# Attention and a squared-ReLU MLP on one core: the first pair in token halves, values behind scores, and more of the first product in batch 1

## The chip, the cores and the metric

The kernel runs on one NeuronCore of one Trainium2 chip. The metric is the device time of one execution in microseconds (us): the median of three runs, and lower is better. Before the change it is 417.86 us (417.58 to 418.33).

A core has five engines that run side by side, each with its own instruction stream that is worked off in order: TensorE (PE, matrix products; its weight loads are listed as PEld), VectorE (DVE, elementwise work), ScalarE (ACT, the exponentials), GpSimd (POOL) and SyncE (SP). The last two mostly issue transfers here. TensorE writes into PSUM, a small memory from which VectorE and ScalarE read; everything else lies in SBUF.

## The reference, cut to what matters

```python
batch, n_heads, seq, head_dim = (8, 12, 448, 64)
n_tokens, d_model, d_ff = (3584, 768, 2048)

def _attn_ref(q, k, v):
    scale = 1.0 / np.sqrt(q.shape[-1])
    scores = scale * np.matmul(q, k.transpose(0, 1, 3, 2))
    m = np.max(scores, axis=-1, keepdims=True)
    e = np.exp(scores - m)
    attn = e / (np.sum(e, axis=-1, keepdims=True) + np.exp(-m) + 1e-09)
    return np.matmul(attn, v).astype(np.float32)

def _moe_ref(x, w_in, w_out):
    h = x @ w_in
    r = np.maximum(h, 0.0)
    g = r * r
    return (g @ w_out).astype(np.float32)

# x: the attention's output, heads side by side: (8 * 448, 12 * 64)
```

Multiplied through by exp(m), the attention is exp(s) / (1 + sum exp(s)): the maximum is not needed, and the kernel computes it in this form. The product with `w_in` is called the first product here, the one with `w_out` the second or output product.

## The kernel before

The unit of the attention is a pair of heads [...]. Batch 0 is cut into two query ranges of 192 and 256 tokens, so that its first product can start early: units 0 to 5 are the six pairs with the first range, 6 to 11 the six pairs with the second, 12 to 17 the six pairs of batch 1. From unit 18 on the units run two at a time, with output-product steps between the score visits (the joined stage, batches 2 to 7).

The first three pairs of batch 0 are loaded as fp32 over the queues of SyncE and ScalarE, cast to fp16, and transposed by TensorE. All else arrives over GpSimd's queue, which casts during the transfer. `keep_warm` issues matmuls on zeros whose result nobody reads, so that TensorE's clock rises and stays up.

```python
def cast(b, pr):
    for name in "qk":
        f = flat.tile([P, 2, RUN, D], FP16, name=f"flat{name}")
        if b == 0 and pr == 0 and name == "k":
            nc.scalar.activation(out=f, in_=naturals[name, b, pr], func=AF.Copy)
        else:
            nc.vector.tensor_copy(f, naturals[name, b, pr])
        naturals[name, b, pr] = f

def transposes(b, pr):
    tp = mp_tile(FP16)
    for i, name in enumerate("qk"):
        for s in range(RUN):
            for h in range(2):
                nc.tensor.transpose(...)
    ...
    parts = (0, S // 2, S) if b == 0 and pr == 0 else (0, S)
    for x, y in zip(parts, parts[1:]):
        nc.vector.tensor_copy(qks[b][:, 0:2, pr * S + x:pr * S + y], tp[:, :, x:y])
```

A unit's scores come in two visits (`scores(u, et, 0)` and `scores(u, et, 1)`), each with half of the keys; the exponentials (ScalarE) follow from one of two PSUM buffers. `values` is the product of the exponentials with v; its result lies in `xp`, of which there is one buffer. `row_sums` adds up the exponentials on TensorE and makes the reciprocal on ScalarE (a Ln and an Exp). `normalise` multiplies the two on VectorE and so frees `xp`.

The first product is queued as tiles of single steps; `drain(ns)` issues steps until their nominal time is used up, `run(ins, n)` issues the rest of n tiles. The end of a tile is two VectorE instructions (maximum with 0, square). Up to the joined stage `mp` tiles rotate in three PSUM buffers.

```python
for i in range(2 * NPAIR):                      # units 0 to 11
    ...
    scores(u, et, 0)
    if i == 0:
        keep_warm(4)
    if i == NPAIR:
        values(units[i - 1], ...); rcp = row_sums(...); normalise(two, xp, rcp)
        queue(0, FIRST)
        share[0] = left() / (NPAIR + 2)
    if i in transpose_at:
        transposes(*transpose_at[i])
    if i == 0:
        cast(0, 2)
    if i > NPAIR:
        drain(share[0] * 0.45)
    scores(u, et, 1)
    if 0 < i < NPAIR:
        keep_warm(1)
    if i and i != NPAIR:
        ... row_sums, values(units[i - 1], ...)
    if i > NPAIR:
        drain(share[0] * 0.3)
    ... add_chunks, normalise, drain(share[0] * 0.25)

for i in range(2 * NPAIR, 3 * NPAIR):           # units 12 to 17
    ...
    scores(u, et, 0)
    if i in transpose_at:
        transposes(*transpose_at[i])
    ... (loads and staging of later batches)
    drain(left() * 0.5 if first else share[0] * 0.45)
    scores(u, et, 1)
    ... row_sums, values of the unit before
    drain(share[0] * 0.15)
    for step in range(3):
        add_chunks(u, et, es, half, step)
        drain(share[0] * (0.15, 0.1, 0.15)[step])
    ...
    normalise(done, xp, rcp)
    if first:
        queue(FIRST, S - FIRST)
        share[0] = left() / (NPAIR + 1.5)

# joined stage, two units a turn
    scores(ua, ea, 0); rows(11); scores(ua, ea, 1); ...; rows(11)
    scores(ub, eb, 0); ...; rows(10); scores(ub, eb, 1); ...
    for at in pending:
        if at not in rcps:
            rcps[at] = row_sums([units[at]], ...)      # first turn: unit 17
        values(...); normalise(...)
    ... transposes of two pairs of batch 2
    if pr == 0:
        run(ins, len(ins))                             # what is left of batch 0
        queue((b - 1) * S, S)
```

Of the kernel before, what the change touches and what calls it, by code (L numbers as in the profile page):

```python
# [15 lines left out]
def kernel(  # L16
# [9 lines left out]
    nc = tc.nc  # L26
# [45 lines left out]
    win_r = moe_w_in.rearrange("(c p) f -> p c f", p=128)  # L72
    wout_r = moe_w_out.rearrange("(c p) f -> p c f", p=128)

    whole, vns, qks, xts, naturals, stages = {}, {}, {}, {}, {}, {}

    def load_v(b, p0, p1):
# [5 lines left out]
    def load_natural(b, p0, p1):  # L83

        raw = b == 0 and p1 <= 3
        for n, r in (("q", q_r), ("k", k_r)):
            src = r[b, :, 2 * p0:2 * p1]
            if raw:
                if p0 == 0:
                    whole[n] = e_pool.tile([P, RUN * S], FP32, name="et")  # L90
                t = whole[n][:, p0 * 512:(p0 + 1) * 512].rearrange("p (h t d) -> p h t d", h=2, t=RUN)
                (nc.sync if n == "q" else nc.scalar).dma_start(out=t, in_=src)
            else:
                if p0 % 3 == 0:
                    whole[n] = nat.tile([P, NPAIR, RUN, D], FP16, name=f"{n}n{p0 // 3}")
                t = whole[n][:, 2 * (p0 % 3):2 * (p0 % 3 + p1 - p0)]
                nc.gpsimd.dma_start(out=t, in_=src)
            for pr in range(p0, p1):
                naturals[n, b, pr] = t[:, 2 * (pr - p0):2 * (pr - p0) + 2]
# [39 lines left out]
            )  # L139


    def cast(b, pr):
        for name in "qk":
            f = flat.tile([P, 2, RUN, D], FP16, name=f"flat{name}")
            if b == 0 and pr == 0 and name == "k":
                nc.scalar.activation(out=f, in_=naturals[name, b, pr], func=AF.Copy)
            else:
                nc.vector.tensor_copy(f, naturals[name, b, pr])
            naturals[name, b, pr] = f

    def transposes(b, pr):
        tp = mp_tile(FP16)
        for i, name in enumerate("qk"):
            for s in range(RUN):
                for h in range(2):
                    nc.tensor.transpose(tp[64 * h:64 * h + 64, i, P * s:P * s + P],
                                        naturals[name, b, pr][:, h, s, :], ident[0:P, 0:P])
        if b not in qks:
            qks[b] = qk_pool.tile([128, 3, COLS], FP16, name="qk")
        parts = (0, S // 2, S) if b == 0 and pr == 0 else (0, S)  # L160
        for x, y in zip(parts, parts[1:]):
            nc.vector.tensor_copy(qks[b][:, 0:2, pr * S + x:pr * S + y], tp[:, :, x:y])

# [226 lines left out]
    def left():  # L392
        return sum(t[0] for t in ins)
# [9 lines left out]
    def drain(ns):  # L403
        while ins and ns > 0:
            ns -= one(ins)
# [10 lines left out]

    transpose_at = {pr - 1: (0, pr) for pr in range(1, NPAIR)}
    for pr in range(NPAIR):
        transpose_at[NPAIR + 3 + pr] = (1, pr)
    transpose_at[16], transpose_at[17] = (2, 0), (2, 1)  # L420

    def keep_warm(n):
        wp = m_psum.tile([128, 512], FP32, name="mp")
        for _ in range(n):
            nc.tensor.matmul(wp, warm[:, 0:128], warm, start=True, stop=True)
# [15 lines left out]
        ess[i] = (es, half)  # L441
        return units[i], ets[i], es, half

    keep_warm(9)
    cast(0, 0)
    transposes(0, 0)
    keep_warm(3)
    cast(0, 1)


    for i in range(2 * NPAIR):
        u, et, es, half = begin(i)
        two = units[i - 2:i] if i and i % 2 == 0 else None
        if i % 2:
            xp = x_psum.tile([128, 512], FP32, name="xp")
        mode[0] = COLS2
        scores(u, et, 0)
        if i == 0:
            keep_warm(4)
        if i == NPAIR:  # L460
            values(units[i - 1], ets.pop(i - 1), xp, units[i - 1][3])
            rcp = row_sums(two, (ess.pop(i - 2)[0:1], ess.pop(i - 1)[0:1]))
            normalise(two, xp, rcp)
            queue(0, FIRST)
            share[0] = left() / (NPAIR + 2)
        if i in transpose_at:
            transposes(*transpose_at[i])
        if i == 0:
            cast(0, 2)
        if i > NPAIR:  # L470
            drain(share[0] * 0.45)
        scores(u, et, 1)
        if 0 < i < NPAIR:
            keep_warm(1)
        if i and i != NPAIR:
            if two and i < NPAIR:
                rcp = row_sums(two, (ess.pop(i - 2)[0:1], ess.pop(i - 1)[0:1]))
            values(units[i - 1], ets.pop(i - 1), xp, (i - 1) % 2 * units[i - 1][3])
            if two and i > NPAIR:
                rcp = row_sums(two, (ess.pop(i - 2)[0:1], ess.pop(i - 1)[0:1]))  # L480
        if i > NPAIR:
            drain(share[0] * 0.3)
        add_chunks(u, et, es, half, 1)
        if two and i != NPAIR:
            normalise(two, xp, rcp)
        add_chunks(u, et, es, half, 2)
        if i > NPAIR:
            drain(share[0] * 0.25)
        if i == NPAIR + 5:
            load_natural(2, 0, 3)  # L490
            for j in range(2):
                load_wout(0, j, 2)


    for i in range(2 * NPAIR, 3 * NPAIR):
        u, et, es, half = begin(i)
        prev = units[i - 1]
        first = i == 2 * NPAIR
        if not first:
            xp = x_psum.tile([128, 512], FP32, name="xp")  # L500
        mode[0] = COLS2
# [3 lines that stand above are left out]
        if i == 2 * NPAIR + 2:  # L505
            load_natural(2, 3, 6)
            for j in range(2):
                load_wout(HALF, j, 2)
            load_v(2, 0, 6)
            stage(3)  # L510
        drain(left() * 0.5 if first else share[0] * 0.45)
        scores(u, et, 1)
        if first:
            done = units[i - 2:i]
            values(prev, ets.pop(i - 1), xp, prev[3])
            rcp = row_sums(done, (ess.pop(i - 2)[0:1], ess.pop(i - 1)[0:1]))
        else:
            done = [prev]
            rcp = row_sums(done, (ess.pop(i - 1)[0:1],))
            values(prev, ets.pop(i - 1), xp)  # L520
        drain(share[0] * 0.15)
        for step in range(3):
            add_chunks(u, et, es, half, step)
            drain(share[0] * (0.15, 0.1, 0.15)[step])
        if i == 3 * NPAIR - 1 and ins and ins[0][0] < ins[0][1]:
            run(ins)
        normalise(done, xp, rcp)
        if first:
            queue(FIRST, S - FIRST)
            share[0] = left() / (NPAIR + 1.5)  # L530

# [11 lines left out]
    for c in range((NU - 3 * NPAIR) // 2):  # L545
        i = 3 * NPAIR + 2 * c
        b, pr = units[i][0:2]
        new = []
        for j in range(2):
            new.append(begin(i + j))  # L550
        (ua, ea, sa, ha), (ub, eb, sb, hb) = new
        scores(ua, ea, 0)
        rows(11)
        scores(ua, ea, 1)
        add_chunks(ua, ea, sa, ha, 0)
        rows(11)
        scores(ub, eb, 0)
        add_chunks(ua, ea, sa, ha, 1)
        add_chunks(ua, ea, sa, ha, 2)
        rows(10)  # L560
        scores(ub, eb, 1)
        add_chunks(ub, eb, sb, hb, 0)
        mode[0] = COLS2
        for at in pending:
            if at not in rcps:
                rcps[at] = row_sums([units[at]], (ess.pop(at)[0:1],))
            xp = mp_tile()
            values(units[at], ets.pop(at), xp)
            normalise([units[at]], xp, rcps.pop(at))
        add_chunks(ub, eb, sb, hb, 1)  # L570
        add_chunks(ub, eb, sb, hb, 2)
        if b in ON_PE and pr + 2 < NPAIR:
            transposes(b, pr + 2)
            transposes(b, pr + 3)
        if pr == 0:
            run(ins, len(ins))
            queue((b - 1) * S, S)
            if b > 2:
                run(outs)
            if b + 1 < B:  # L580
                transposed_loads(b + 1)
                hold(b + 1)
                load_v(b + 1, 0, NPAIR)
                if b + 2 < B:
                    stage(b + 2)

        n, early = ((3, 0 if b > 2 else 1), (7, 3), (6, 3))[pr // 2]
        run(ins, early)
        for at in (i, i + 1):
            rcps[at] = row_sums([units[at]], (ess.pop(at)[0:1],))  # L590
        run(ins, n - early)
        if pr == NPAIR - 2:
            complete(b * S)
        pending = [i, i + 1]
# [38 lines left out]
```

## Time and profile before

| | before |
|---|---|
| time, median of 3 | 417.86 us |
| span of the profiled execution | 415.9 us |
| TensorE busy | 405.5 us (98%) |
| VectorE busy | 278.8 us (67%) |
| ScalarE busy | 238.4 us (57%) |
| first exponential starts | 7.03 us |
| first exponential of unit 6 starts | 20.40 us |
| joined stage begins (scores of unit 18) | 67.35 us |
| last first-product steps of batch 0 | from 76.60 us |

A stretch of the profile gives each engine's busy time between two moments; the difference from the stretch's length is the engine's idle time. A line of a timeline gives the start and length of one or several instructions of the same kind, the tile written and the tiles read, the number of instructions, and in brackets how long the engine had been idle before and what released it. Matmuls are pipelined and their ends are modelled, so costs of TensorE are taken from differences of starts. The chain of waits is followed back from the last instruction: each of its pieces is what released the next. A transfer's line shows its issue; its landing is given separately, as the time from issue to landing.

### The profile page before, as it was taken

How to read it: one execution, taken by the hardware profiler on the slowest of the kernel's cores; microseconds unless marked ns; L12 is line 12 of the kernel's file. 1: busy time of each engine (PE TensorE's matmuls, PEld its weight loads, DVE VectorE, ACT ScalarE, POOL GpSimd, SP SyncE). 2: the span in 40 equal slices, each digit the busy share in tenths (PEclk: the TensorE clock that was granted, in tenths of full speed). 3: DMA queues.
4: the chain of work that ended last, by engine and by line, in shares of the span. 5: the costliest groups of instructions: out<-in, count | busy, mean ns of one | idle time of the engine just before them, and what ended most of it. 6: DMA issues, size and time to landing. Idle time of an engine off the chain costs nothing.

```text
span 415.9 us, 10695 instructions
## 1 busy us (share of the span) xinstructions
PE 405.5 (98%) x4721; PEld 256.7 (62%) x4721; DVE 278.8 (67%) x535; ACT 238.4 (57%) x329; POOL 36.4 (9%) x58
## 2 busy tenths in 40 slices
PE   8889999899999999999999999999999999999997
PEld 3567666566566666665666666665666666555664
DVE  4769888768865868568766769658676669287000
ACT  4897998664675664673576564674666655100111
POOL 7523220020000200002000400001000000000000
PEclk9999999999999999999999999999999999999999
DMA  9999999889109790199509871198101101010222
GB/s 201 197 197 198 200 197 223 159 120 199 40 2 182 139 192 6 44 199 191 123 2 164 167 151 37 39 186 154 46 2 39 39 2 39 39 39 0 77 76 77
DMA packets 75823, 45.58 MB, mean 110 GB/s; under 512 B 42560, under 2 KB 72000, under 8 KB 75456
## 3 DMA queue, kind: packets, MB, share of 16 engines
q0 software_dynamic: 28848, 22.16, 35.0%
q1 hardware_dynamic: 46208, 22.05, 23.3%
q8 instruction: 37, 0.61, 0.6%
q10 hardware_dynamic: 720, 0.69, 0.6%
q14 instruction: 10, 0.08, 0.1%
HBM read 45.69 MB, written 17.93 MB: 153 GB/s over the span
## 4 chain that ended last, share of the span: by engine, by line
PE 86%; DMA 9%; ACT 2%; DVE 2%; issue 1%; POOL 0%; POOLq 0%
PE mp L284 23%; PE mp L330 17%; PE mp L286 11%; PE xp L284 8%; PE sp L199 6%; PE xp L330 6%; PE mp L234 5%; DMA kn<-in_k_dram 4%; PE xp L286 3%; DMA win<-in_moe_w_in_dram 3%; PE xp L234 3%; PE sp L187 2%; DMA vn<-in_v_dram 2%; PE mp L248 2%; ACT et L167 1%
## 5 line engine op out<-in xcount | busy, mean ns | idle before, releaser
L167 ACT ACTIVATE et<-sp 112x896 f16<-112x896 f32 (+2 forms) x192 | 165.8, 914 | 55.6 <-PE sp L199 40.1
L284 PEld LDWEIGHTS <-win 128*64 128x64 f16 x1536 | 85.3, 110 | 45.7 <-issue 2.8
L284 PE MATMUL mp<-xt,win 128*64 128x448 f16 (+2 forms) x1236 | 110.2, 324 | 1.5 <-DVE xt L263 0.8
L330 PE MATMUL mp<-wout,gs 64*128 64x384 f16 x864 | 102.3, 322 | 0.0
L330 PEld LDWEIGHTS <-gs 64*128 64x128 f16 x1152 | 56.1, 94 | 31.7
L301 DVE TENSOR_SCALAR rt<-mp 128x448 f16<-128x448 f32 (+2 forms) x99 | 61.6, 622 | 17.4 <-PE mp L284 13.3
L303 DVE TENSOR_TENSOR gs<-rt 128x448 f16<-128x448 f16 (+2 forms) x128 | 50.2, 392 | 4.4
L330 PE MATMUL xp<-wout,gs 64*128 64x384 f16 x288 | 52.6, 322 | 0.0
L251 ACT ACTIVATE rcp<-mp,one_b 128x448 f32<-128x448 f32 (+2 forms) x40 | 25.1, 629 | 40.1 <-PE mp L248 35.8
L212 DVE TENSOR_TENSOR es<-et 112x896 f16<-112x896 f16 x42 | 26.0, 620 | 17.7 <-ACT et L167 17.6
L339 ACT ACTIVATE ot<-mp 128x384 f32<-128x384 f32 (+1 forms) x29 | 14.1, 487 | 36.2 <-PE mp L286 27.6
L199 PE MATMUL sp<-qk 64*112 64x224 f16 x480 | 33.8, 260 | 0.0
L286 PEld LDWEIGHTS <-gs 128*128 128x128 f16 x256 | 24.4, 98 | 15.1 <-issue 0.4
L284 PE MATMUL xp<-xt,win 128*64 128x448 f16 x300 | 32.6, 352 | 0.0
L199 PEld LDWEIGHTS <-qk 64*112 64x112 f16 x480 | 26.3, 128 | 9.7 <-issue 5.4
L234 PEld LDWEIGHTS <-vn 112*64 112x64 f16 x432 | 22.1, 109 | 15.3 <-issue 5.2
L286 PE MATMUL mp<-wout,gs 128*128 128x384 f16 (+1 forms) x192 | 31.0, 322 | 0.0
L341 DVE SCALAR_TENSOR_TENSOR ot<-mp,ot 128x384 f32<-128x384 f32 x27 | 15.1, 558 | 21.7 <-PE sp L199 11.6
L252 ACT ACTIVATE rcp<-rcp 128x448 f32<-128x448 f32 (+2 forms) x48 | 27.7, 577 | 1.5
L214 DVE TENSOR_TENSOR es<-es,half 112x896 f16<-112x896 f16 x42 | 26.2, 625 | 1.4
L212 DVE TENSOR_TENSOR half<-et 112x896 f16<-112x896 f16 x42 | 25.9, 616 | 0.3 <-ACT et L167 0.3
L301 DVE TENSOR_SCALAR rt<-xp 128x448 f16<-128x448 f32 x29 | 18.0, 622 | 12.0 <-PE xp L286 8.3
(61 smaller groups left out, 313.9 us busy)
## 6 DMA issues: line engine op xcount, KB each, us to landing
vn<-in_v_dram POOLq DMA_DIRECT2D x7, 672.0 KB, 9.0
out_dram<-ot SPq DMA_DIRECT2D x9, 384.0 KB, 2.8
win<-in_moe_w_in_dram POOLq DMA_DIRECT2D x8, 384.0 KB, 13.9
wout<-in_moe_w_out_dram POOLq DMA_DIRECT2D x4, 768.0 KB, 12.8
stage_q<-in_q_dram POOLq DMA_DIRECT2D x4, 676.0 KB, 10.9
stage_k<-in_k_dram POOLq DMA_DIRECT2D x4, 676.0 KB, 13.3
out_dram<-ot SPq DMA_DIRECT2D x8, 288.0 KB, 3.2
out_dram<-ot SPq DMA_DIRECT2D x9, 192.0 KB, 2.7
```

Source lines behind the costliest of these rows:

```text
L167: nc.scalar.activation(out=out_, in_=in_, func=AF.Exp, scale=scale)
L199: nc.tensor.matmul(sp[:, odd, h * (S // 2):(h + 1) * (S // 2)], qk[r, which, kx:kx + 2 * P - 1:2], qk[r, 0, x:x + S // 2], start=True, sto ...
L212: nc.vector.tensor_add((es, half[:, 0:2 * S])[step], e[:, 2 * step], e[:, 2 * step + 1])
L214: nc.vector.tensor_add(es, es, half[:, 0:2 * S])
L234: nc.tensor.matmul(xp[64 * h:64 * h + 64, o:o + n], vns[b][:, 2 * pr + h, kk, :], of_head(chunk(et, u, kk // 2, kk), u, h), start=(kk == 0 ...
L251: nc.scalar.activation(out=rcp[:, 0:m], in_=zp[:, 0:m], func=AF.Ln, bias=one_b)
L252: nc.scalar.activation(out=rcp[:, 0:m], in_=rcp[:, 0:m], func=AF.Exp, scale=-1.0)
L284: nc.tensor.matmul(out_[x:x + 64], lhsT[:, x:x + 64], rhs, start=start, stop=stop)
L286: nc.tensor.matmul(out_, lhsT, rhs, start=start, stop=stop)
L301: nc.vector.tensor_scalar(out=rt[:, 0:m], in0=hp[:, 0:m], scalar1=0.0, scalar2=None, op0=ALU.max)
L303: nc.vector.tensor_mul(gs[:, f0:f0 + per, t0 % RING:t0 % RING + n], r, r)
L330: nc.tensor.matmul(o[:, 0:w], g[x:x + 64], wout[x:x + 64, fb, n0:n0 + w], start=(fb == 0), stop=(fb == NFFB - 1))
```

## The change

It is meant to take idle time out of TensorE in the stages before the joined stage.

- Pair 0 is loaded, cast, transposed and copied in two halves of the tokens, so that the first scores need only the first half. Pair 2's keys move from ScalarE's queue to SyncE's. The casts of pair 1's keys move to ScalarE. There are four warm-up matmuls fewer.
- The values of units 2 and 4 are issued one unit later, after the next unit's first scores, so that scores don't stand behind values that wait for `xp`.
- Units 7 to 11 and 12 get fewer first-product steps, units 13 to 17 more, above all between the two score visits; batch 0's first product ends with unit 17, as do the row sums of unit 17. Two tiles of batch 1 instead of one then stand ahead of the first turn's row sums.
- Batch 1's pairs 3 to 5 are transposed one unit later.

```diff
+    HALVES = ((0, RUN // 2), (RUN // 2, RUN))
@@ load_natural
-                (nc.sync if n == "q" else nc.scalar).dma_start(out=t, in_=src)
+                for s0, s1 in HALVES if p0 == 0 else ((0, RUN),):
+                    eng = nc.sync if n == "q" or p0 == 2 else nc.scalar
+                    eng.dma_start(out=t[:, :, s0:s1], in_=src[:, :, s0:s1])
@@ cast, transposes: both take s0, s1
-            if b == 0 and pr == 0 and name == "k":
+            if pr < 2 and name == "k":
-        parts = (0, S // 2, S) if b == 0 and pr == 0 else (0, S)
+        for x, y in HALVES if b == 0 and pr == 1 else ((s0, s1),):
@@ before the loops
-        transpose_at[NPAIR + 3 + pr] = (1, pr)
+        transpose_at[NPAIR + 3 + pr + pr // 3] = (1, pr)
-    keep_warm(9)
-    cast(0, 0)
-    transposes(0, 0)
-    keep_warm(3)
-    cast(0, 1)
+    keep_warm(8)
+    cast(0, 0, *HALVES[0])
+    transposes(0, 0, *HALVES[0])
+    cast(0, 0, *HALVES[1])
+    keep_warm(2)
@@ units 0 to 11
         if i == 0:
-            keep_warm(4)
+            transposes(0, 0, *HALVES[1])
+            cast(0, 1)
+            keep_warm(1)
+            scores(u, et, 1)
+            keep_warm(1)
+        if two and i in (4, NPAIR):
+            values(two[0], ets.pop(i - 2), xp)
-            share[0] = left() / (NPAIR + 2)
+            share[0] = left() / (NPAIR + 4)
-        scores(u, et, 1)
+        if i:
+            scores(u, et, 1)
-            values(units[i - 1], ets.pop(i - 1), xp, (i - 1) % 2 * units[i - 1][3])
+            if i not in (3, 5):
+                values(units[i - 1], ets.pop(i - 1), xp, (i - 1) % 2 * units[i - 1][3])
@@ units 12 to 17
-        drain(left() * 0.5 if first else share[0] * 0.45)
+        before = 0.65 if i in transpose_at else 0.8
+        drain(share[0] * (1.2 if first else before))
-        drain(share[0] * 0.15)
+        after = 0.5 if first else 1.0 - before
+        drain(share[0] * after * 0.4)
-            drain(share[0] * (0.15, 0.1, 0.15)[step])
-        if i == 3 * NPAIR - 1 and ins and ins[0][0] < ins[0][1]:
-            run(ins)
+            drain(share[0] * after * 0.2)
+        if i == 3 * NPAIR - 1:
+            run(ins, len(ins))
+            rcps[i] = row_sums([u], (ess.pop(i)[0:1],))
-            share[0] = left() / (NPAIR + 1.5)
+            share[0] = left() / (NPAIR - 0.2)
@@ joined stage
-            if at not in rcps:
-                rcps[at] = row_sums([units[at]], (ess.pop(at)[0:1],))
-            run(ins, len(ins))
-        n, early = ((3, 0 if b > 2 else 1), (7, 3), (6, 3))[pr // 2]
+        n, early = ((3, 0 if b > 2 else 2), (7, 3), (6, 3))[pr // 2]
```

More of the change, by code (lines that the diff above doesn't have):

```diff
@@ L139, in transposed_loads, with cast, transposes @@
             )
-    def cast(b, pr):
+    fp16s = {}
+    def cast(b, pr, s0=0, s1=RUN):
         for name in "qk":
-            f = flat.tile([P, 2, RUN, D], FP16, name=f"flat{name}")
-            if b == 0 and pr == 0 and name == "k":
-                nc.scalar.activation(out=f, in_=naturals[name, b, pr], func=AF.Copy)
-            else:
-                nc.vector.tensor_copy(f, naturals[name, b, pr])
-            naturals[name, b, pr] = f
-    def transposes(b, pr):
+            if s0 == 0:
+                fp16s[name, b, pr] = flat.tile([P, 2, RUN, D], FP16, name=f"flat{name}")
+            f, t = fp16s[name, b, pr][:, :, s0:s1], naturals[name, b, pr][:, :, s0:s1]
+            if pr < 2 and name == "k":
+                nc.scalar.activation(out=f, in_=t, func=AF.Copy)
+            else:
+                nc.vector.tensor_copy(f, t)
+    def transposes(b, pr, s0=0, s1=RUN):
         tp = mp_tile(FP16)
[L153 to L157, printed above, removed]
         if b not in qks:
             qks[b] = qk_pool.tile([128, 3, COLS], FP16, name="qk")
-        parts = (0, S // 2, S) if b == 0 and pr == 0 else (0, S)
-        for x, y in zip(parts, parts[1:]):
-            nc.vector.tensor_copy(qks[b][:, 0:2, pr * S + x:pr * S + y], tp[:, :, x:y])
+        for i, name in enumerate("qk"):
+            for s in range(s0, s1):
+                for h in range(2):
+                    t = fp16s.get((name, b, pr), naturals[name, b, pr])
+                    nc.tensor.transpose(tp[64 * h:64 * h + 64, i, P * s:P * s + P], t[:, h, s, :], ident[0:P, 0:P])
+        for x, y in HALVES if b == 0 and pr == 1 else ((s0, s1),):
+            nc.vector.tensor_copy(qks[b][:, 0:2, pr * S + P * x:pr * S + P * y], tp[:, :, P * x:P * y])
     def exp(out_, in_):
```

## The prediction, made before the changed kernel ran

> **What bounds the kernel now.** I read four views in this order: busy time in stretches (where TensorE has gaps), TensorE's own timeline (what it waits for), the chain of waits (which transfers it passes through), and ScalarE's timeline. First the stretches; the columns are the stretch, its length, then the busy time of PE, PEld, DVE, ACT and POOL, the clock, the DMA share and GB/s.
>
> ```profile
> 5.05:19.90 14.85, 13.13 (x205) 7.88 (x204) 10.59 (x23) 11.35 (x17) 9.15 (x12) 1.00 1.41 207
> 19.90:27.86 7.96, 6.79 (x111) 4.91 (x108) 4.73 (x10) 7.42 (x10) 2.77 (x4) 1.00 1.45 197
> 42.00:67.35 25.35, 23.70 (x341) 16.23 (x338) 21.92 (x42) 23.84 (x33) 5.28 (x7) 1.00 1.38 206
> 67.35:83.11 15.76, 14.57 (x188) 9.51 (x186) 11.79 (x22) 10.69 (x15) 0.00 (x0) 1.00 0.87 177
> 83.11:355.60 272.49, 272.49 (x3267) 172.68 (x3266) 199.45 (x379) 164.83 (x226) 12.05 (x22) 1.00 0.49 96
> ```
>
> From 83.11 us on TensorE has no gap at all until the tail, and the change leaves that work as it is. So the time is what the first 83 us take, plus a constant, and only gaps, warm-up matmuls or work shifted within those 83 us can matter. Before that three engines take turns: ScalarE is busy 23.84 of 25.35 us while batch 1 runs alone. TensorE's timeline shows how it waits there and just after (start, length, instruction, idle before it):
>
> ```profile
> 19.48 0.52 PE L234 MATMUL xp<-et,vn 112*64 112x192 f16 x8 [0.79 <-DVE xt L263]
> 38.42 0.39 PE L156 MATMUL mp<-ident,kn 112*64 112x112 f16 x8 [0.28 <-DMA kn<-in_k_dram]
> 44.32 0.40 PE L187 MATMUL sp<-qk 64*112 64x448 f16 x2 [0.45 <-ACT et L167]
> 76.60 2.64 PE L284 MATMUL mp<-xt,win 128*64 128x256 f16 x36 [0.46 <-ACT rcp L251]
> ```
>
> The values wait behind a normalise, batch 1's second load arrives late, scores wait for a buffer that an exponential still reads, and after 75 us the last first-product tiles of batch 0 are all TensorE has while it waits for unit 17's row sums. The chain of waits shows that the loads form a second path through the first 38 us:
>
> ```profile
> 10.31 12.93 DMA win<-in_moe_w_in_dram
> 23.82 14.56 DMA kn<-in_k_dram
> ```
>
> The stretches have the DMA engines full at some 197 GB/s up to 42 us, so a faster start can't bring later data earlier. Landings, from the issues of short windows: keys of batch 1's first half at 26.8 us, of its second half at 38.4, its values at 41.9 (25.75 plus 16.1).
>
> [...] The first warm-ups here start 0.43 us apart, the three at 5.87 us take 0.82 together[...] Both queues already moved about half each of 340 GB/s between 3 and 5.2 us. [...]
>
> **Unit costs, from starts in TensorE's timeline.** One first-product step (two 64-column matmuls side by side): at 192 columns 12 matmuls go from 28.66 to 29.28, 0.103 us a step; at 256 columns 22 from 46.42 to 47.72, 0.118; at 448 columns 24 from 109.25 to 111.52, 0.189. A full set of transposes 0.42 (34.64 to 35.06), a half of batch 1's scores 0.52, values 0.75, row sums 0.22. On ScalarE a unit of batch 1 costs 4 exponentials at 0.87, a Ln and an Exp at 1.24: 4.7, and the units stand 4.81 apart (48.16 to 52.97).
>
> **Part 1, halves.** The first pair's queries are cast at 4.49, the first exponential starts at 7.03. With halves and 8 warm-ups TensorE is free at 1.20 + 8 x 0.427 = 4.62; the first half should have landed by then (4.45 now; half of both tensors is 229 KB less ahead of it, 0.67 us at the 340 GB/s of those two queues, so about 3.8). Transposes to 5.05, a half copy of 0.35 (two take 0.69 now), two warm-ups beside it, scores at 5.5, exponential at about 5.9: 1.1 earlier. The second starts at about 7.3 instead of 8.82, because the whole pair's second half no longer waits for VectorE's casts. Then the gain shrinks. Pair 2's casts, two half copies and unit 0's sums all queue on VectorE; its copy of pair 2 ends at about 10.6, against 11.2, so unit 2 starts 0.6 earlier. Four warm-ups fewer save 4 x 0.22, but they stood in waits.
>
> **Part 2, values behind scores.** At unit 6 it lets scores pass the 0.79 us wait, but ScalarE was idle for only 0.17 there. At unit 4 it may hurt: the values ran at 14.97 while TensorE would have waited for pair 4's copy anyway (scores at 15.77); now 0.44 of values stand between unit 4's two score visits, and I expect a ScalarE gap of up to 0.5. I keep **0.3 us** of gain at 20 us.
>
> **Part 3, fewer steps early.** Counting whole steps (a drain overshoots to a whole step): units 7 to 11 go from 13 to 11 each, unit 12 from 24 to 17, units 13 to 17 from 91 to 120, and the 12 left for after 75 us go to none. The sum is 192 in both. Units 7 and 8 are on ScalarE's path (its gaps there are under 0.2), units 9 to 11 on TensorE's (ScalarE gaps of 0.52, 0.55 and 0.53), so 10 steps, 1.03 us, bring 0.8: unit 12 starts at 37.23 - 1.1 = 36.1. Unit 12 lasts 4.78 now. It loses 7 steps (0.72), the transposes moved to unit 13 (0.42) and their wait (0.28): 3.4, so unit 13 starts at 39.5, after the 38.4 landing.
>
> **Part 4, batch 1 filled.** Unit 13: scores 1.04, transposes 0.42, 24 steps at 0.103, 4 at 0.118, values and sums 0.97: 5.4, with 0.4 of waits for exponentials 5.8, to 45.3. Units 14 to 16: 0.52 + 0.42 + 13 x 0.118 + 0.52 + 0.22 + 0.75 + 9 x 0.118 = 5.03 each, over ScalarE's 4.7, so TensorE becomes the bound and its waits go: 60.4. Unit 17 has 4 steps more, its own row sums and a wait for them: 5.8. The joined stage starts at 66.2, against 67.35: **1.15 earlier, with the 12 left-over steps already done**.
>
> **Part 5, joined stage.** It takes 15.76 us now. Its work to the end of the transposes is 8.8; less the row sums 8.6. Then two 448-column tiles, row sums, a third tile: 2 x 1.14 + 0.44 + 1.14 = 3.9. That is 12.5; I add 0.4, because ScalarE enters with two more Ln and Exp just before its exponentials. 12.9 instead of 15.76: 1.42 of steps gone, 0.22 of sums, and 1.2 of gaps (0.46, 0.35, 0.15, 0.22) as unit 17's reciprocal no longer queues behind eight exponentials. It ends at 79.1 instead of 83.1. Sum: **4 us less**, 417.86 - 4.0 = 413.9; I say 414.0.
>
> **Rivals.** (a) The loads bind. If the start gained more than 1.5 us, unit 9's transposes (28.27 now) would wait for the 26.8 landing; and unit 13's values, at about 43.3, cannot start before 41.9. So nothing brings the total down by more than about 1.4 us beyond my figure: about 412.4. For it: full DMA engines up to 42 us. Against: my start gains too little to reach it. (b) VectorE becomes the bound in batch 1. Per unit it has three adds at about 0.58, one normalise and one transposed copy at 0.54 each, and 1.83 tiles at 1.07 (51.99 to 53.06): 4.8 of 5.03 us. Because sums wait for the last exponential, tile evictions queue behind them, and with three rotating buffers TensorE could stall 0.2 to 0.4 per unit: 415 to 416. For it: 21.92 of 25.35 us busy already. (c) Longer drains between score visits starve ScalarE, and units stay at 4.8 plus the excess: 0.3 each, 1.5 in all: 415.5. Against: with 1.2 us of Ln and Exp still ahead of the next exponential, scores arrive early enough. (d) The second natural load of batch 2 waits for transposes one unit later and delays the second weight half. Against: the queue has work until 53.1, and the issue moves by about 1 us only; no change.
>
> **Range and chances.** (b), (c) and a lost start can each cost 1 to 1.5 us; (a) caps the other side at about 412.4, and my start and gap terms may be off by 0.7. So 411.8 to 416.4. A gain over 2% needs 8.4 us; the stretches from 5.05 to 83.11 hold 6.2 us of TensorE gaps in all (1.72 + 1.17 + 0.15 + 0.28 + 1.65 + 1.19), and the four warm-ups 0.9; a loss over 2% would need a new stall of 12 us. 0.02, 0.96, 0.02.
>
> **What would show it.** First exponential near 5.9 and second near 7.3; unit 6's first exponential 0.3 earlier than 20.40; no wait for keys at 38 us; units 14 to 16 about 5.0 apart with no TensorE wait for exponentials; no 256-column step after the first output product; the joined stage 12.9 long; the gapless stretch from about 79. The prediction is wrong if units of batch 1 stand over 5.3 apart, if unit 6 starts late, or if the gap after unit 17 persists in another form.

## The result, and the profile after

The changed kernel takes 421.5 us (median of 4 executions, 420.69 to 422.64) against 417.97 us for four of the kernel before (417.58 to 418.33): a ratio of 1.0087, 95% interval 1.0057 to 1.0116. It is slower by nearly 1%, where 414.0 was predicted and 411.8 to 416.4 given as the range.

The same stretches as before the change, from the changed kernel (stretch, length, busy time of PE, PEld, DVE, ACT and POOL, granted clock, DMA share, GB/s):

```profile
5.05:19.90 14.85, 12.60 (x136) 7.00 (x132) 7.54 (x18) 7.29 (x10) 8.70 (x11) 0.68 1.38 209
19.90:27.86 7.96, 6.78 (x81) 4.42 (x79) 4.12 (x9) 5.84 (x8) 3.30 (x4) 0.74 1.45 197
42.00:67.35 25.35, 24.99 (x400) 18.36 (x398) 23.47 (x46) 22.82 (x31) 7.73 (x10) 1.00 1.01 142
67.35:83.11 15.76, 13.68 (x180) 9.82 (x180) 10.66 (x20) 12.26 (x18) 0.00 (x0) 1.00 1.15 196
83.11:355.60 272.49, 272.33 (x3286) 172.84 (x3284) 199.77 (x379) 165.63 (x228) 11.77 (x22) 1.00 0.52 101
```

Read the clock column first: it was 1.00 in every stretch before, and is now 0.68 and 0.74 in the first two. In the first stretch TensorE is busy for 12.60 us with 136 matmuls, where it needed 13.13 us for 205. The stretches lie at the same times as before, but the work in them has moved: unit 12, the first of batch 1, starts at 42.89 us instead of 37.23, so the third line is batch 1 up to unit 16, and the fourth holds unit 17 and the start of the first joined turn. The third is fuller than before, 24.99 of 25.35 us. Finer stretches show where the clock goes:

```profile
9.00:10.00 1.00, 0.00 (x0) 0.00 (x0) 0.00 (x0) 0.47 (x1) 0.00 (x0) 1.00 1.35 227
10.00:11.00 1.00, 0.51 (x8) 0.29 (x8) 0.24 (x1) 0.86 (x2) 0.00 (x0) 0.67 1.42 203
12.00:24.00 12.00, 12.00 (x130) 7.47 (x130) 6.59 (x15) 7.40 (x10) 6.95 (x9) 0.50 1.46 197
24.00:25.00 1.00, 1.00 (x19) 0.66 (x15) 0.53 (x1) 0.83 (x2) 0.00 (x0) 1.00 1.45 196
```

TensorE stands still from 9 to 10 us; then the clock falls to one half, at 10.34 us, and stays there until 23.99. What it stood still for is in its timeline and in ScalarE's, in one piece of the chain of waits (start, length, what), and in the transfer's line, first of the kernel before, then of the changed one (size, time from issue to landing):

```profile
9.53 0.63 ACT L153 ACTIVATE flatk<-et 112x512 f16<-112x512 f32 x1 [1.91 <-DMA et<-in_k_dram]
10.07 0.79 ACT L172 ACTIVATE et<-sp 112x768 f16<-112x768 f32 x1
10.21 0.51 PE L165 MATMUL mp<-ident,flatk 112*64 112x112 f16 x8 [1.53 <-ACT flatk L153]
```

```profile
1.73 7.78 DMA et<-in_k_dram
```

```profile
et<-in_k_dram ACTq DMA_DIRECT2D x1, 224.0 KB, 5.2
et<-in_k_dram ACTq DMA_DIRECT2D x1, 224.0 KB, 7.8
```

Pair 1's keys, issued at 1.73 us, land at 9.5. Before, the same transfer took 5.2 us from an issue at about 1.2, so it landed at 6.4, and the transposes of these keys stood here in TensorE's timeline:

```profile
8.11 0.36 PE L156 MATMUL mp<-ident,flatk 112*64 112x112 f16 x8
```

ScalarE works in order: the cast of these keys, which the change put there, holds up unit 0's second exponential as well (10.07, predicted 7.3). It ends at 10.86, before the next scores start at 11.21, so it costs TensorE nothing; the late transposes do.

The second thing to see is at the end of batch 1, in TensorE's timeline, ScalarE's and VectorE's:

```profile
74.41 0.38 PE L253 MATMUL mp<-es,ones 112*64 112x448 f16 x2 [1.67 <-DVE es L219]
70.11 1.72 ACT L172 ACTIVATE et<-sp 112x896 f16<-112x896 f32 x2 [0.67 <-PE sp L192]
```

```profile
71.48 0.69 DVE L306 TENSOR_SCALAR rt<-mp 128x512 f16<-128x512 f32 x1 [1.35 <-PE mp L289]
72.20 0.42 DVE L308 TENSOR_TENSOR gs<-rt 128x512 f16<-128x512 f16 x1
72.55 0.62 DVE L217 TENSOR_TENSOR es<-et 112x896 f16<-112x896 f16 x1
73.08 0.62 DVE L217 TENSOR_TENSOR half<-et 112x896 f16<-112x896 f16 x1
73.73 0.63 DVE L219 TENSOR_TENSOR es<-es,half 112x896 f16<-112x896 f16 x1
```

Unit 17's row sums, now issued before the joined stage, wait 1.67 us for VectorE's three adds. These stand in VectorE's order behind a first-product tile that VectorE itself waits 1.35 us for, so the adds begin only at 72.55. The last two exponentials of the unit end at 71.83. Had the first add, which needs only the first two, run before that and the other two right after it, some 0.4 us of the wait would have been left (an estimate: 71.83 plus the 1.3 us from the second add to TensorE's start, less the 72.74 at which TensorE began to wait).

### The profile page after: what moved, and what is told of

Read it like the earlier page. It is cut to its first block, busy times and chain, and to the rows that moved or that the text cites. A ratio compares the mean times of both kernels' runs of the same rounds, so it can differ in the third digit from the quotient of the medians.

```text
span 420.9 us, 10694 instructions
## 1 busy us (share of the span) xinstructions
PE 409.7 (97%) x4717; PEld 260.2 (62%) x4717; DVE 278.5 (66%) x536; ACT 238.9 (57%) x331; POOL 36.2 (9%) x58
## 4 chain that ended last, share of the span: by engine, by line
PE 89%; DVE 4%; ACT 4%; DMA 2%; issue 1%; ACTq 0%
PE mp L289 24%; PE mp L335 16%; PE mp L291 10%; PE xp L289 7%; PE sp L204 6%; PE xp L335 6%; PE mp L239 5%; PE xp L239 4%; PE xp L291 4%; PE sp L192 3%; ACT et L172 2%; PE mp L253 2%; DMA et<-in_k_dram 2%; PE mp L165 2%; DVE qk L167 1%
## 5 line engine op out<-in xcount | busy, mean ns | idle before, releaser
L289 PE MATMUL mp<-xt,win 128*64 128x448 f16 (+2 forms) x1260 | 111.8, 324 | 0.8 <-DVE xt L268 0.8
L306 DVE TENSOR_SCALAR rt<-mp 128x448 f16<-128x448 f32 (+2 forms) x101 | 62.7, 621 | 23.8 <-PE mp L289 11.6
L335 PEld LDWEIGHTS <-gs 64*128 64x128 f16 x1152 | 57.1, 94 | 30.6
L344 ACT ACTIVATE ot<-mp 128x384 f32<-128x384 f32 (+2 forms) x29 | 13.9, 480 | 55.3 <-PE mp L291 44.2
L256 ACT ACTIVATE rcp<-mp,one_b 128x448 f32<-128x448 f32 (+2 forms) x38 | 23.9, 628 | 34.2 <-PE mp L253 34.2
L291 PEld LDWEIGHTS <-gs 128*128 128x128 f16 x256 | 24.4, 98 | 15.1 <-issue 0.4
L289 PE MATMUL xp<-xt,win 128*64 128x448 f16 x276 | 30.0, 352 | 0.1
L291 PE MATMUL mp<-wout,gs 128*128 128x384 f16 (+2 forms) x192 | 29.6, 313 | 0.0
L346 DVE SCALAR_TENSOR_TENSOR ot<-mp,ot 128x384 f32<-128x384 f32 x27 | 15.1, 558 | 18.9 <-PE sp L204 9.6
L192 PE MATMUL sp<-qk 64*112 64x448 f16 (+2 forms) x192 | 25.4, 342 | 2.1 <-ACT et L172 1.4
```

The lines of the kernel that those rows point to most:

```text
L192: nc.tensor.matmul(sp[:, h, o:o + n], qk[r, 1, x + P * kk:x + P * kk + P], qk[r, 0, x + q0:x + q0 + n], start=True, stop=True)
L289: nc.tensor.matmul(out_[x:x + 64], lhsT[:, x:x + 64], rhs, start=start, stop=stop)
L291: nc.tensor.matmul(out_, lhsT, rhs, start=start, stop=stop)
L306: nc.vector.tensor_scalar(out=rt[:, 0:m], in0=hp[:, 0:m], scalar1=0.0, scalar2=None, op0=ALU.max)
L335: nc.tensor.matmul(o[:, 0:w], g[x:x + 64], wout[x:x + 64, fb, n0:n0 + w], start=(fb == 0), stop=(fb == NFFB - 1))
```

## The experiments

Two questions were asked. Why does the start fail: is it the move of pair 2's keys, the halves, their short rows, or GpSimd's queue; and is it the late data or the clock that costs the time? And what are the other parts worth, where the sum of them promised nearly 4 us? All ratios are to the kernel before, with 95% intervals.

### Pair 2's keys back on ScalarE's queue

```diff
-                    eng = nc.sync if n == "q" or p0 == 2 else nc.scalar
+                    eng = nc.sync if n == "q" else nc.scalar
```

> The changed kernel, with pair 2's keys back on ScalarE's queue; pair 0 still in halves. In the changed kernel pair 1's keys landed at 9.53 us, TensorE stood idle for 1.53 us before them, and its clock was at half from about 10.7 to 24 us. Theory Q (the fourth and fifth load on SyncE's queue take the engines' turns from ScalarE's queue): pair 1's keys land near 6.5, no idle time over 1 us before 10 us, clock stays full, 415 us. Theory H (the halves double the number of rows of 512 bytes, so the two fast queues run dry or lag and GpSimd's queue comes in at 3.7 instead of 5.4): still near 9.5, half clock, 421 us.

Measured: 421.39 us, ratio 1.0082 (1.0054 to 1.011). Pair 1's keys land 7.9 us after an issue at about 1.7, as late as in the changed kernel, and the clock is 0.65 in the stretch from 5.05 to 20 us. Theory Q falls: moving the one transfer does nothing.

### Pair 0 loaded whole

```diff
-                for s0, s1 in HALVES if p0 == 0 else ((0, RUN),):
+                for s0, s1 in ((0, RUN),):
```

> The changed kernel, with pair 0 loaded whole (one transfer for q, one for k); casts, transposes and copies still in halves, pair 2's keys still on SyncE's queue. Theory H (the halves delay what follows): pair 0 lands near 4.5 and 4.9, pair 1's keys near 6.5, GpSimd's queue comes in at about 5.4, clock stays full, first exponential near 6.4, 414 to 415.5 us. Theory Q (the queue move): pair 1's keys still after 9, half clock, 420 to 421 us.

Measured: 417.07 us, 0.9993 (0.9972 to 1.0014). Pair 1's keys land 5.0 us after an issue at about 1.2, at 6.2; the clock is full in the profiled execution; GpSimd's first packets come at 5.2 us as before (5.4), not at 3.8. So the halved load alone brings the 4.4 us, and the rest of the new start, casts and copies in halves and four warm-ups fewer, makes no difference to the median. The first scores start at 6.08 us, but unit 6 at 20.02, against 19.94 in the kernel before. Of the 20 executions 16 took 416.74 to 417.51 us at full clock and two 418.33 and 418.49 at a mean clock of 0.996. The other two took 422.31 and 422.39, with a recorded clock of 1.0 and 0.999; no trace of them was kept, and their cause is open.

### Halves by head instead of by token

```diff
-                for s0, s1 in HALVES if p0 == 0 else ((0, RUN),):
-                    eng.dma_start(out=t[:, :, s0:s1], in_=src[:, :, s0:s1])
+                for h0, h1 in ((0, 1), (1, 2)) if p0 == 0 else ((0, 2),):
+                    eng.dma_start(out=t[:, h0:h1], in_=src[:, h0:h1])
```

> The changed kernel with pair 0 loaded in two halves by head instead of by token: as many transfers as in the changed kernel, but rows of 1024 bytes, as many rows as before. Theory R (the rows of 512 bytes, twice as many, delay what follows in the two fast queues): pair 1's keys land near 6.5, GpSimd's queue comes in after 5, clock full, about 417 us. Rival T (the number of transfers and their order do it): pair 1's keys after 9, half clock in most executions, 420 to 421.5 us. Casts and transposes of half the tokens need both heads, so the first exponential is no earlier than with the pair loaded whole.

Measured: 421.31 us, 1.0079 (1.005 to 1.0108). The rows are as long and as many as before, and still pair 1's keys take 7.3 us from an issue at about 1.7, landing near 9, where they take 5.0 with the pair loaded whole. Theory R falls: it is not the short rows but the splitting into more transfers, which makes pair 1's the third in their queues instead of the second.

### GpSimd's loads held until pair 1's keys have landed

```diff
-    load_v(0, 0, 3)
     ident = consts.tile([128, 128], FP16)
     make_identity(nc, ident)
+    landed = consts.tile([1, 1, 1, 1], FP32)
+    nc.gpsimd.tensor_copy(landed, naturals["k", 0, 1][0:1, 0:1, 0:1, 0:1])
+    load_v(0, 0, 3)
```

> The changed kernel with GpSimd's loads held back until pair 1's keys have landed (a one-element copy on GpSimd reads them); the loads of the two fast queues are unchanged. In both loads by halves the third transfer of each fast queue crawled, and GpSimd's packets came in just then (from 3.6 to 3.8 us, against 5.2 to 5.4 with pair 0 loaded whole). Theory P (GpSimd's packets take the turns): pair 1's keys land by about 6 us. Rival S (the third transfer of a fast queue is slow by itself, whoever else runs): they land after 8.5 us also with GpSimd's queue empty. The total says little, as all later data come later: 419 to 423 us.

Measured: 421.27 us, 1.0087 (1.0069 to 1.0104); the keys land 6.0 us after an issue at about 1.7, at 7.7. That lies between the two theories. Of the 3.1 us of lateness (9.5 against 6.4), GpSimd's packets explain 1.8. The other 1.3 us are there with GpSimd's queue empty, and the trace shows two slow places. Between 3.6 and 4.0 us, just after the four half transfers, both fast queues together move only 0.03 MB, where 0.4 us moved 0.12 before. And between 5 and 7 us SyncE's queue (q1) gets nearly all, while the last of pair 1's keys trickle in over ScalarE's (q10); packets, MB, share of the 16 engines:

```profile
q1 hardware_dynamic: 427, 0.41, 92.0%
q10 hardware_dynamic: 83, 0.07, 14.4%
```

SyncE's queue holds pair 2's keys here. Taking them off it did nothing while GpSimd's packets ran (7.9 us for pair 1's keys, against 7.8); with GpSimd's queue empty this was not tried. The cause of the 1.3 us is left open.

### Warm-up matmuls through the gap

```diff
             scores(u, et, 1)
-            keep_warm(1)
+            keep_warm(8)
```

> The changed kernel with seven more warm-up matmuls just ahead of pair 1's transposes, so that TensorE works while pair 1's keys are late; the loads are untouched, so the lateness itself stays. Theory C (the idle time costs most through the clock): the clock stays full, unit 6 starts near 22 instead of 26.0, total about 417.5 us. Rival (the late keys cost the time directly, the half clock is little beside it): unit 6 near 25 to 26, total 421 us or a little more.

Measured: 418.88 us, 1.0056 (1.0034 to 1.0079). Its first two stretches have their clock back:

```profile
5.05:19.90 14.85, 12.87 (x183) 7.02 (x180) 9.05 (x21) 8.99 (x13) 8.47 (x11) 1.00 1.37 207
19.90:27.86 7.96, 5.83 (x91) 4.18 (x87) 3.98 (x8) 7.47 (x11) 3.37 (x5) 1.00 1.45 197
```

The loads are as late as in the changed kernel, and yet 2.6 us are won by seven matmuls on zeros. The single executions show it more sharply, because seven matmuls did not always suffice: 12 of 20 had a mean clock of 0.999 or 1.0 and took 418.21 to 419.05 us, 8 had one of 0.984 to 0.988 and took 421.73 to 423.45. The half clock costs 3.9 us (422.5 less 418.6, the medians of the two groups), with the same instructions. A mean of 0.984 over 420 us is 13.4 us at half clock, which agrees with the 0.50 from 10.34 to 23.99 us above. In the changed kernel all four executions had 0.984 to 0.992, and so had all ten of the three versions before this one with the load in halves; of 91 executions of the kernel before only two fell below 0.999 (421.4 us at 0.984, 422.93 at 0.98). What is left at full clock, 418.6 against 416.9 with the pair loaded whole (medians of the executions at 0.999 or 1.0, without the two of 422 us), is the direct cost of the late keys: about 1.7 us.

### The old start with all the later parts

The edit puts the loads, casts, transposes and warm-ups of the first pairs back as they were and keeps everything else.

> The kernel before with all of the change but its start: loads, casts, transposes and warm-ups of the first pairs as before; values behind scores, fewer steps early, more steps in batch 1, row sums of unit 17 early. Theory: these parts work as predicted, and only the start failed: 413.5 to 414.5 us, unit 6 near 20.4, joined stage from about 67, gapless from about 79.5. Rival (VectorE or starved exponentials hold batch 1 up, or the wait of 1.67 us for unit 17's sums, seen in the changed kernel, eats it): 416 to 417 us.

Measured: 416.98 us, 0.9978 (0.9964 to 0.9993): the later parts bring 0.8 us, not nearly 4. The wait for unit 17's sums is here too, TensorE's timeline:

```profile
68.92 0.38 PE L249 MATMUL mp<-es,ones 112*64 112x448 f16 x2 [1.66 <-DVE es L215]
```

From unit 6 on this kernel and the changed one have the same lengths, to a few hundredths of a microsecond, in every stage; they differ in when unit 6 begins. So each stage can be set against the prediction (durations in us, from the first score visit of one unit to that of another; predicted ones from the terms of the prediction):

| stage | before | predicted | measured |
|---|---|---|---|
| units 6 to 11 | 17.29 | 16.5 | 16.87 |
| unit 12 | 4.78 | 3.4 | 3.73 |
| unit 13 | 5.71 | 5.8 | 5.42 |
| units 14 to 16 | 14.43 | 15.1 | 15.18 |
| unit 17 | 5.20 | 5.8 | 7.50 |
| first joined turn | 15.76 | 12.9 | 13.52 |
| sum | 63.17 | 59.5 | 62.22 |

### Unit 17's row sums where they were

```diff
-            rcps[i] = row_sums([u], (ess.pop(i)[0:1],))
@@ joined stage
         for at in pending:
+            if at not in rcps:
+                rcps[at] = row_sums([units[at]], (ess.pop(at)[0:1],))
```

> Old start plus the later parts (416.98 us), with unit 17's row sums put back to where the kernel before had them, behind the fourth score visit of the joined stage; batch 0's first product still ends with unit 17. Theory W (the early sums cost 1.66 us of TensorE idle time that the joined stage gives back only in part): the joined stage starts about 1.8 us earlier, but its first tile of batch 1 now waits some 1 to 1.5 us for the normalise behind eight exponentials: 416.0 to 417.0 us. Rival (the early sums are a clear net gain, they save the old 0.46 + 0.35 us of gaps and more): 417.5 us or more.

Measured: 416.45 us, 0.9964 (0.9952 to 0.9977): 0.5 us better than with the early sums. The early sums were a loss, but about half of the 2.05 us that their removal saves (unit 17 takes 5.45 us instead of 7.50) is given back in the joined turn, which takes 14.61 instead of 13.52.

### Unit 17's row sums in the middle

```diff
         rows(11)
+        for at in pending:
+            if at not in rcps:
+                rcps[at] = row_sums([units[at]], (ess.pop(at)[0:1],))
         scores(ua, ea, 1)
```

> Old start plus the later parts, with unit 17's row sums issued after the first eleven output steps of the joined stage: by then VectorE has the sums, so TensorE does not wait, and the reciprocal is still ahead of the other six exponentials. Theory W (the 1.66 us wait is a loss of order only): the wait goes and nothing takes its place, 415.2 to 415.6 us, 1.4 to 1.8 below 416.98. Rival (ScalarE or VectorE is the bound around the joint, and the wait shows up again at the score visits or tiles of the joined stage): 416.5 us or more.

Measured: 415.77 us, 0.9949 (0.9934 to 0.9963). The sums now come at 69.07 us, behind output steps that began at 67.16, and no idle time stands in the line:

```profile
67.16 1.95 PE L331 MATMUL mp<-wout,gs 64*128 64x384 f16 x22
69.07 0.38 PE L249 MATMUL mp<-es,ones 112*64 112x448 f16 x2
```

1.2 us are won over the early sums: unit 17 takes 5.46, the turn 13.98. Theory W holds for most of the wait; 0.46 us of it comes back in the turn.

### Values where they were

```diff
-        if two and i in (4, NPAIR):
-            values(two[0], ets.pop(i - 2), xp)
-            if i not in (3, 5):
-                values(units[i - 1], ...)
+            values(units[i - 1], ...)
```

> Old start plus the later parts, without values behind scores: units 2 and 4's values stand where the kernel before had them. If the part does what it is for, this is 0.2 to 0.5 us slower than 416.98. If, as the prediction feared, it costs a gap of ScalarE at unit 4, this is 0.2 to 0.5 us faster. If scores at units 4 and 6 wait for ScalarE's buffers anyway (0.94 and 0.90 us in the trace with the part), there is no difference, 416.8 to 417.2.

Measured: 416.55 us, 0.9971 (0.9959 to 0.9982): 0.4 us better without the part in the medians, though single executions overlap (416.13 to 417.08 against 416.46 to 418.19). ScalarE's timeline at unit 4, first with values behind scores, then with values in their old place:

```profile
16.80 0.81 ACT L168 ACTIVATE et<-sp 112x768 f16<-112x768 f32 x1 [0.46 <-PE sp L188]
17.94 0.81 ACT L168 ACTIVATE et<-sp 112x768 f16<-112x768 f32 x1 [0.34 <-PE sp L188]
```

```profile
16.45 1.63 ACT L168 ACTIVATE et<-sp 112x768 f16<-112x768 f32 x2 [0.46 <-PE sp L188]
```

The first gap of 0.46 us is there either way. The scores of unit 4 then wait for ScalarE's exponential, by the trace, but VectorE's copy of pair 4 ends at the same moment (16.33 us with the part, 15.98 without), so which of the two they wait for isn't shown; it is not the values, which stand behind these scores with the part. With the part a second gap of 0.34 us opens, since the values now stand between the two score visits.

### The corrections together

Old start, values in their old place, row sums in the middle:

> Old start, values where they were before, fewer steps early and more in batch 1, unit 17's row sums after the first eleven output steps. The gains of the two corrections were 1.2 us (415.77 against 416.98) and 0.4 us (416.55 against 416.98); if they add, 415.3 us, 2.4 below the kernel before. If one hides the other (ScalarE's gap at unit 4 is caught up by unit 9 anyway), 415.8 us.

Measured: 415.33 us, 0.9940 (0.9928 to 0.9953). The two corrections add, as the first case said. The same with the rest of the new start (casts, transposes and copies of pair 0 in halves, fewer warm-ups, pair 2's keys on SyncE's queue), the pair loaded whole:

> As the version just above, but with the start of the changed kernel (casts, transposes and copies of pair 0 in halves, pair 1's keys cast on ScalarE, eight and two warm-ups), pair 0 loaded whole. The prediction gave this start 0.3 us at unit 6. If so, 415.0 us, 0.3 below the version above. If the halves of the casts are worth nothing without the early landing, the same within 0.2 us. If fewer warm-ups let the clock drop in some executions, some of them lie 4 to 5 us above the rest.

Measured: 415.04 us, 0.9943 (0.9932 to 0.9954). The two can't be told apart. One of the latter's 20 executions had a mean clock of 0.983 and took 419.17 us; the others lie between 414.56 and 416.26. Both beat the kernel before and the changed one.

## Why the prediction was wrong, point by point

The prediction missed by 7.5 us (421.5 less 414.0). In the profiled execution 6.4 of this lie before unit 6, which started at 26.02 us where 19.64 was expected, and 2.7 in the stages up to the end of the first joined turn (62.22 less 59.5). That is 9.1; the profiled execution, at 422.64 us and so 8.6 above the prediction, was the slowest of the four. Two of the signs that the prediction named for being wrong came: unit 6 started late, and the gap after unit 17 persisted in another form.

**The step that failed is part 1, the halves.** Its first term was right and even cautious: the first half was cast at 3.38 us, where a landing at 3.8 was worked out. What it did not ask is what four transfers in place of two do to the transfer behind them. The working has no landing for pair 1, so this was left where the kernel before had it; it came 3.1 us later. The sentence that a faster start "can't bring later data earlier" looked in one direction only. Two consequences follow. TensorE resumes 2.1 us later than before (10.21 against 8.11, the transposes of pair 1's keys). And the clock falls after this gap, so that the work from there to unit 6 takes 15.8 us instead of 11.8: another 4.0. Together these are the 6.1 us by which unit 6 is late. The runs show the two separately: full clock by warm-ups is worth 3.9, data on time a further 1.7.

**The warm-ups were mis-sized as well.** "Four warm-ups fewer save 4 x 0.22, but they stood in waits" counted their time and not what they are for. The two beside the first copy were taken at the warm 0.22 each; in the profile they take 1.03 us together, as the first two of all do (from 1.20), where two of the kernel before take 0.60 from 5.87. By these lengths the clock had not risen yet, and the first exponential comes at 6.82 instead of 5.9. (The clock column reads 1.00 there; the cold start shows only in the lengths of the matmuls.) When the clock rises differed between two executions: with one and the same start unit 0's scores stand at 6.62 us in the profile of the kernel before, behind transposes of 0.39 us for a tensor, and at 7.23 in that with the later parts, behind transposes of 0.58. In the changed kernel it then fell: it went to 0.50 behind a gap of 1.53 us in sparse work (TensorE busy 1.71 of the 3.41 us before, 6.93 to 10.34), and 12 us of unbroken busy time passed before it rose. No rival in the prediction mentions the clock.

**Part 2** was sized nearly right in its doubt: "a ScalarE gap of up to 0.5" at unit 4 is 0.34, and taking the part out brings 0.4 us. The 0.3 of gain at unit 6 that was kept in spite of it was not there.

**Part 3** had the mechanism right. Units 6 to 11 gained 0.42 us where 0.8 was worked out, and unit 12 took 3.73 instead of 3.4, as its second scores still wait 0.19 us for an exponential. No wait for keys at 38 us remained, as expected.

**Part 4** was right for units 14 to 16: 15.18 us for three, or 5.06 each, against 5.03 worked out, and TensorE has no wait for exponentials in them. Rivals (b) and (c) did not come: VectorE kept up. For **unit 17** the term "its own row sums and a wait for them" was sized at about 0.3, of which less than 0.1 for the wait, and measured 1.97, of which 1.66 were the wait. The busy time of VectorE had been added up, but not the order in which its adds stand.

**Part 5** was short by 0.6: 13.52 instead of 12.9, among other things 0.41 us of waiting for a score buffer while ScalarE makes two more reciprocals.

**Rival (a)**, that the loads bind, was right about the resource and wrong about the place. It looked at GpSimd's queue at 27 and 42 us, where it made no difference, and not at the two fast queues at 4 us. (Its cap, 413.9 less 1.4, is 412.5 and not 412.4; nothing hangs on it.) **Rival (d)** did not come, as was argued there: the second weight half made nobody wait.

The sentence that a loss needs "a new stall of 12 us" stands for a loss over 2%; what came was a loss of under 1%, out of a stall of 2 us and the half clock that followed it.

## What to carry to other kernels

Cutting a load in two to start earlier can also delay what stands behind it in its queue (here 7.8 us from issue to landing instead of 5.2): look up when the next transfer's data are needed, and weigh the early half against that. Warm-up matmuls that fill a wait are an insurance against a low clock (here 1.00 instead of 0.68 in the first stretch, in the profiled execution): weigh them by what the clock would cost, not by what they take. Seven of them won 2.6 us in the late gap here, while the new start with four fewer made no difference to the median once the data were on time (417.07 against 416.98 us). Before a result is wanted earlier, read the order of the engine that makes it: its position behind other work on VectorE decided the wait here, and issuing the sums a few steps later was worth 1.2 us.

## What the runs showed of the hardware that was not expected

- A gap of 1.53 us in TensorE's work before 10.2 us was followed by 13.65 us at half clock (10.34 to 23.99), although TensorE was busy without a gap for 12 of them. The price was 3.9 us; whether it was paid varied between executions of one kernel with the gap partly filled (8 of 20).
- The low clock lasted 13.65 us in the changed kernel's profile, and the other times fit multiples of a quarter of it, some 3.41 us. With pair 2's keys back on ScalarE's queue it was some 13.7 us (four), an estimate from clocks of 0.65 over 14.95 us and 0.80 over the next 8.00; with halves by head and with GpSimd held some 10.1 us (three), an estimate from a mean clock of 0.988 over 419.4 and 419.6 us. The mean clocks of the single executions agree: where they are below 0.999, they stand near 0.996, 0.992, 0.988, 0.984 and 0.98, and a step of 0.004 over 420 us is 3.4 us at half clock.
- What brings the clock down stays open. In the changed kernel it fell with TensorE busy 1.71 of the 3.41 us before; in the kernel before it stayed full through 3.41 us with only 2.23 busy (17.90 to 21.31). With GpSimd held a warm-up at 11.12 us still took 0.39 us, and the values at 12.71 took 0.85, where they take 0.52 at full clock in the kernel before. Between 7.45 and 11.12 us TensorE had waited four times, 0.58 us at most and 1.50 in all; it then stood idle for 1.20 us ahead of 12.71, and whether the clock fell before or during this is not shown.
- GpSimd's first load was issued at 1.30 us in the kernels before and changed. Its packets began when ScalarE's queue had moved its first two transfers: at about 5.4 us with pairs 0 and 1 whole, at 3.8 with pair 0 in halves. ScalarE's third transfer then crawled: pair 1's keys, 229 KB, took from 4.2 to 9.2 us, some 46 GB/s, where the two fast queues had moved 310 GB/s together from 2.4 to 3.6. SyncE's third, pair 1's queries, landed 5.4 us after an issue at about 1.7 in the changed kernel. With GpSimd's queue held empty the keys were still late by 1.3 us. The cause of that part stays open.
